# A gated two-branch attention on one core: a scheduled program replaced by one in a stored order, with fewer vector steps and transposes made by DMA

## The chip, the cores and the metric

The kernel runs on one core of one Trainium2 chip. The metric is device microseconds of one execution; lower is better. The engines are named as the profile names them: PE (TensorE), ACT (ScalarE), DVE (VectorE), POOL (GpSimd) and SP, which here only issues DMAs.

## What is computed

Input `x` has 2048 tokens of 640 values; there are 32 heads of 20. Two branches read it and a sigmoid gate mixes them.

```python
# branch A: linear attention, features are softmax(+p) and softmax(-p) of p = head @ w_phi
phi_q = concat([softmax(pq), softmax(-pq)]); phi_k = concat([softmax(pk), softmax(-pk)])
kv = einsum('bhsf,bhsd->bhfd', phi_k, v); z = einsum('bhsf->bhf', phi_k)
a = (phi_q @ kv) / (phi_q . z + 1e-6)  -> @ wo
# branch B: 4 segments of 512 tokens; causal softmax attention inside each segment,
# and a memory M, z summed over the earlier segments with phi(t) = where(t > 0, t + 1, exp(t))
o = g_h * (phi(q) @ M) / (phi(q) . z + 1e-6) + (1 - g_h) * softmax(q k^T * scale + mask) @ v
M = M + phi(k)^T v; z = z + sum(phi(k))   -> @ wo
out = g * a + (1 - g) * b,   g = sigmoid(x . gate_w)
```

## The kernel before

The program is recorded first and issued afterwards. Each call of `Graph.op` (L107) records one operation with an engine or a choice of engines, a guessed duration, a priority `pr`, and the tiles that it reads and writes. `schedule` (L134) then walks the operations greedily: for each engine it takes the candidates that could start within 0.12 us of the earliest one and picks the lowest priority number. In the same walk it hands out the 8 PSUM banks and the SBUF slots. `emit` (L359) writes five instruction streams in that order and places the semaphore waits. Each engine issues its stream strictly in order, so an instruction that waits holds up all that stand behind it.

Work by stages, with the lines that the prediction speaks of:

- Setup (L593): SP transposes `x` and two slices of `wqkv` by DMA while they are loaded, in this order: segment 0 of `x`, `wkT`, the other three segments, `wqT`. ACT's queue loads the rest. `fuse` (L669) multiplies w_phi into the A weights.
- Branch B, four segments n (`b_proj`, L687): the q and k projections (L698, five matmuls of 512 columns for each chunk), the v projection (L719, L720), and a way through DRAM (`scr`) for 12 of every 32 rows, so that 8 head groups of 4 heads lie at partitions 0, 32, 64 and 96.
- For each of the 8 groups (`b_step`, L815): three bursts of logit matmuls (L830; key tile 0, then tiles 1 and 3, then tile 2), five exponentials of 1024 columns (L839, L858), four masks on POOL (L844), and 40 small matmuls with the values (L884). For segments 1 to 3 four more matmuls read the memory in the same step (L887), and `combine` (L893) makes five DVE steps out of it (L906, L908, L916, L930, L933).
- Memory keys (`b_mem`, L746): PE transposes k (L762), ACT and DVE make the features from PSUM (L765, L767, L769).
- Outputs of a segment (`b_out`, L938): PE transposes (L947) and an evacuation each (L682 on ACT, L683 on DVE).
- Branch A keys (`a_k`, `a_kv`): projections (L968, L969), exponentials (L975), a sum per head and its reciprocal (L981, L982), a normalisation on POOL or DVE (L983), the kv matmuls (L999), and a running sum over tokens on DVE (L1022, 64 partitions by 1280).
- Branch A queries (`a_q`, L1062): projections (L1072), exponentials of both signs (L1077), then for each token tile two halves. In each half the two signs are multiplied by kv into two PSUM banks (L1097) and six DVE steps (L1105, L1106, L1107, L1110, L1112, L1113) bring them to one denominator and add them. PE transposes the result (L1122).
- `final` (L1139, L1140): both branches times `Wo`, 512 and 128 columns at a time, and the output DMA.

The core of a branch B step, and of the two signs:

```python
p0 = burst([(0, 0)]); expair(p0, 0, 0); mask(0, ...)
p1 = burst([(1, 0), (3, 384)]); expair(p1, 512, 1); mask(1, ...); mask(3, ...)
p2 = burst([(2, 0)])                       # 256 of 512 columns of each bank used
```

## Time and profile before

| | us |
|---|---|
| median of 3 runs | 446.2 (442.15 to 446.68) |
| span of the profiled execution, first to last instruction | 441.5 |
| PE busy in that span | 335.6 |
| DVE busy | 287.6 |
| ACT busy | 274.3 |
| POOL busy | 131.0 |

The profile is of one execution. Of its own time the page gives the span; the three runs lie 0.65 to 5.2 us above it, the median 4.7. Busy time is the union of an engine's instructions. PE's includes the time in which its clock was granted at half rate.

### The profile page before, as it was taken

What the parts mean: (1) busy time and instruction counts of PE and PEld (TensorE: products, weight loads), DVE (VectorE), ACT (ScalarE), POOL (GpSimd) and SP (SyncE); (2) the same over time, 40 slices, a digit from 0 to 9 for tenths busy, and PEclk for the clock granted to TensorE, in tenths of its full rate; (3) what the DMA queues carried; (4) which work ended last, traced back from release to release, by engine and by line L of the source; (5) the groups of instructions that cost most, each with busy time, mean ns of one, the idle gap of its engine ahead of it and who ended that gap; (6) DMA issues with size and microseconds to landing.
All of it is one profiled execution on the core that took longest, in us unless ns stands there. A gap on an engine that the chain in (4) does not pass through costs nothing.

```text
span 441.5 us, 8777 instructions
## 1 busy us (share of the span) xinstructions
PE 335.6 (76%) x3716; PEld 197.5 (45%) x3762; DVE 287.6 (65%) x584; ACT 274.3 (62%) x356; POOL 131.0 (30%) x163
## 2 busy tenths in 40 slices
PE   0198889596697788686878797877898688867667
PEld 0144454443373446344336454544545364534343
DVE  1321597957866868799428878778733598648940
ACT  1147858565646874577594577678487846477622
POOL 8100643423414441655120122132222212142310
PEclk9999999888698898699689999799898859865569
DMA  8993100410000000044100014000000000000001
GB/s 223 275 189 44 48 3 3 78 27 0 1 16 1 1 0 16 2 150 75 31 0 3 0 25 97 16 16 16 16 30 4 1 1 31 16 15 2 1 1 59
DMA packets 25799, 16.97 MB, mean 38 GB/s; under 512 B 17665, under 2 KB 23585, under 8 KB 25761
## 3 DMA queue, kind: packets, MB, share of 16 engines
q1 hardware_dynamic: 23040, 13.11, 13.4%
q10 hardware_dynamic: 2624, 3.28, 2.3%
q8 instruction: 29, 0.48, 0.4%
q0 software_dynamic: 96, 0.04, 0.2%
q14 instruction: 10, 0.07, 0.1%
HBM read 6.92 MB, written 4.59 MB: 26 GB/s over the span
## 4 chain that ended last, share of the span: by engine, by line
PE 44%; DVE 38%; ACT 9%; DMA 3%; issue 3%; POOL 1%; SPq 1%; POOLq 0%; ACTq 0%
PE ps L698 7%; PE ps L1139 7%; PE ps L968 5%; DVE acc L1022 5%; PE ps L1072 5%; ACT expT L839 4%; PE ps L884 4%; DVE cb L930 4%; DVE z L981 3%; DMA wkT<-in_A_wqkv_dram 3%; PE ps L719 3%; PE ps L1140 2%; DVE W L1110 2%; DVE W L1107 2%; PE ps L830 2%
## 5 line engine op out<-in xcount | busy, mean ns | idle before, releaser
L844 POOL TENSOR_SCALAR_AFFINE_SELECT expT<-expT 128x512 bf16<-128x512 bf16 x128 | 88.9, 697 | 266.5 <-ACT expT L839 216.1
L839 ACT ACTIVATE expT<-ps 128x1024 bf16<-128x1024 f32 x128 | 124.3, 1023 | 31.7 <-PE ps L830 31.5
L884 PE MATMUL ps<-v1B,expT 128*128 128x21 bf16 x1280 | 42.3, 175 | 10.5 <-POOL expT L844 8.0
L698 PE MATMUL ps<-xT,WB 128*128 128x512 bf16 x188 | 49.1, 402 | 1.3 <-issue 0.5
L884 PEld LDWEIGHTS ps<-v1B,expT 128*128 128x128 bf16 x1280 | 39.5, 98 | 18.5 <-POOL expT L844 11.1
L830 PE MATMUL ps<-qk 20*128 20x128 bf16 (+3 forms) x512 | 38.8, 338 | 8.8 <-ACT expT L839 5.8
L858 ACT ACTIVATE expT<-ps 128x1024 bf16<-128x1024 f32 x32 | 32.7, 1022 | 10.9 <-PE ps L830 10.9
L983 POOL TENSOR_TENSOR E<-E,z 128x1280 bf16<-128x1280 bf16 x12 | 30.0, 2496 | 21.9 <-DVE z L982 19.0
L1022 DVE TENSOR_TENSOR acc<-acc,E 64x1280 bf16<-64x1280 bf16 x31 | 31.6, 1018 | 0.8
L968 PE MATMUL ps<-WvA,xT 128*128 128x512 bf16 x74 | 26.7, 443 | 4.7 <-DVE cb L930 3.3
L1072 PE MATMUL ps<-xT,WqA 128*128 128x512 bf16 x95 | 27.9, 443 | 2.8 <-ACT expT L858 1.1
L698 PEld LDWEIGHTS ps<-xT,WB 128*128 128x128 bf16 x200 | 19.0, 102 | 23.1 <-issue 6.0
L1077 ACT ACTIVATE ET<-ps 128x512 bf16<-128x512 f32 x40 | 23.2, 600 | 8.5 <-PE ps L1072 8.1
L1097 PE MATMUL ps<-KVZ,ET 128*128 128x154 bf16 x192 | 20.7, 262 | 9.7 <-DVE W L1110 4.5
L682 ACT ACTIVATE out<-ps 128x640 bf16<-128x640 f32 x13 | 9.2, 704 | 29.5 <-PE ps L1140 29.5
L975 ACT ACTIVATE E<-ps 128x640 bf16<-128x640 f32 x32 | 22.6, 707 | 7.3 <-PE ps L969 7.0
L981 DVE TENSOR_REDUCE z<-E 128x64 f32<-128x1280 bf16 x16 | 23.6, 1478 | 4.9 <-ACT E L975 4.7
L682 ACT ACTIVATE qk<-ps 128x512 bf16<-128x512 f32 x29 | 17.3, 599 | 14.4 <-PE ps L698 13.5
L968 PE MATMUL ps<-WkA,xT 128*128 128x512 bf16 x73 | 23.5, 403 | 3.2 <-DVE vA L683 1.2
L1139 PE MATMUL ps<-Wo,oTA 128*128 128x512 bf16 x71 | 24.1, 422 | 1.1 <-DVE W L1110 1.1
L719 PE MATMUL ps<-WvB,xT 128*128 128x512 bf16 x75 | 23.5, 394 | 1.9 <-ACT v1B L682 1.1
L830 PEld LDWEIGHTS ps<-qk 20*128 20x128 bf16 x512 | 10.5, 94 | 31.7 <-ACT expT L839 13.2
(119 smaller groups left out, 655.5 us busy)
## 6 DMA issues: line engine op xcount, KB each, us to landing
out_dram<-out SPq DMA_DIRECT2D x16, 160.0 KB, 3.4
scr<-qk SPq DMA_DIRECT2D x16, 120.0 KB
qk<-scr SPq DMA_DIRECT2D x16, 120.0 KB
stq<-in_B_wq_dram ACTq DMA_DIRECT2D x1, 800.0 KB, 4.8
stk<-in_B_wk_dram ACTq DMA_DIRECT2D x1, 800.0 KB, 9.6
WvB<-in_B_wv_dram ACTq DMA_DIRECT2D x1, 800.0 KB, 11.6
...
```

Of the source, the lines that this page charges most:

```text
L698: r = e.matmul(self.pf(pt, 0, 0, LSEG), lhsT=self.WB[:, w, kc, 128 * c:128 * (c + 1)], rhs=xT[:, kc, LSEG * n:LSEG * (n + 1)], start=(kc = ...
L719: e.matmul(self.pf(pt, 0, 0, 512), lhsT=l, rhs=self.WvB[:, kc, 0:512], start=(kc == 0), stop=(kc == 4))
L830: r = e.matmul(self.pf(pt, i, c0, N), lhsT=qk[32 * i:32 * i + DH, g, 1, 128 * j:128 * (j + 1)], rhs=qk[32 * i:32 * i + DH, g, 0, 128 * j:L ...
L839: self.op("act", d_act(1024), lambda e, p=p: e.activation(ex[:, 2 * p:2 * p + 2, off:off + 512], self.pbanks(pt, 2 * p, 2, 512), ACT.Exp, ...
L844: self.op("pool", d_pool(n_el), lambda e: e.affine_select(view(), view(), pattern=pat, compare_op=ALU.is_ge, fill=0.0, base=0, channel_mul ...
L858: return e.activation(ex[:, :, 1024:1280].rearrange("p (k b) c -> p k b c", k=2), src, ACT.Exp, scale=scale)
L884: r = e.matmul(self.pf(ad, b, 84 * q2 + 21 * i, 21), lhsT=ex[:, i, c0:c0 + 128], rhs=vt[:, j, h, :], start=(j == 0), stop=(j == qi), skip_ ...
L968: e.matmul(self.pf(pt, 0, 0, 512), lhsT=l, rhs=W[:, kc, 0:512], start=(kc == 0), stop=(kc == 4))
L981: self.op("dve", d_dve(1280), lambda e: e.tensor_reduce(z[:, :], Ev(), axis=AX.X, op=ALU.add), R=[(E, 0), (E, 1)], W=[(z, "*")], claim=[rz ...
L1022: self.op("dve", d_dve(1280, 2), lambda e, src=src: e.tensor_tensor(acc[lo:lo + 64, :], acc[lo:lo + 64, :], src(), ALU.add), R=[(self.Et[t ...
L1072: r = e.matmul(self.pf(pt, 0, 0, LSEG), lhsT=self.WqA[:, kc, 128 * c:128 * (c + 1)], rhs=xT[:, kc, LSEG * S:LSEG * (S + 1)], start=(kc == ...
L1139: e.matmul(self.pf(pt, 0, 0, 512), lhsT=l, rhs=self.Wo[:, c, 0:512], start=(c == 0), stop=(c == 9))
```

## The change

The whole program is written anew. What it does, part by part:

- **Order.** `schedule` and all guessed durations are gone. `replay` takes three tables: `ORDER` (the 1317 operations in one sequence), `ENGINE` (which engine each operation with a choice gets) and `PLACE` (the PSUM banks and SBUF slots). The waits follow from the dependences as before.
- **Start.** Twelve matmuls on a zero tile come first on PE. SP's first transfer is segment 1 of `x`, and PE's first real work is its v projection; the B weights are rearranged in 20 small copies on DVE, ACT and POOL.
- **Key tile 2** of two head groups goes in one burst (`b_pair`), into one 512-column bank per head: two exponentials of 1024 columns and one mask of 1024 for both groups; tiles 1 and 3 share one mask. 80 bursts and 80 masks stand in place of 96 and 128.
- **Memory.** It is read once per token tile for all heads (`b_ret`), with three DVE steps and one addition on DVE or POOL, no longer in each group's step. The head gate sits in the mask `Mm` and in the ones column of the values, so the group's step keeps two DVE instructions.
- **Transposes by DMA.** The memory keys (15 transfers of 128x512), the outputs of branch B (16 of 128x640) and of branch A (16 of 128x640) are turned by transfers on SP's queue. The 256 PE transposes and their evacuations are gone.
- **Branch A's signs in one tile.** 40 matmuls with a 0/1 matrix sum the exponentials per head, DVE divides the two sums, the quotient is spread over the rows of its head through DRAM (four writes and one read on SP), and the negative sign's exponentials are multiplied by it. Both signs then add up in one PSUM tile; three DVE steps per token tile stand in place of twelve.
- **Running sum.** The token sums of branch A are done per sign (64 partitions by 640), and 31 of 64 go to POOL. The gate `1 - g` is applied in the output's evacuation.

```diff
-    def schedule(self):
-        free = {s: 0.0 for s in STREAMS}
-        bank_occ = [None] * 8
...
+    def replay(self, order, engine, place):
+        assert sorted(order) == list(range(len(self.ops)))
+        self.order = [self.ops[i] for i in order]
+        for p, o in enumerate(self.order):
+            o.pos = p
+            o.stream = o.engs[0]
+        for o, e in zip([o for o in self.ops if len(o.engs) > 1], engine):
+            o.stream = o.engs[e]
+        for o in self.order:
...
+                pl = place[t.idx]
+                if t.pool == "psum":
+                    t.t = list(pl)
...
-        p0 = burst([(0, 0)])
-        expair(p0, 0, 0)
-        mask(0, lambda: ex[:, :, 0:128], [[0, 4], [1, 128]], 512, [(0, 0), (0, 1)])
-        p1 = burst([(1, 0), (3, 384)])
-        expair(p1, 512, 1)
-        mask(1, lambda: ex[:, :, 512:640], [[0, 4], [1, 128]], 512, [(1, 0), (1, 1)])
-        mask(3, lambda: ex[:, :, 896:1024], [[0, 4], [1, 128]], 512, [(1, 0), (1, 1)])
...
-        self.op("act", d_act(1024), exp2, W=[(p2, i) for i in range(4)] + [(ex, 2)], pr=s + 0.02, name="exp2")
...
+    def b_pair(self, n, ga, gb):
+        exC = self.sbt("exC", [128, 4, 2, 256], BF16, self.p_exC)
+        pc = self.burst(n, [(ga, 2, 0), (gb, 2, 256)])
+        self.expm(pc, lambda p: exC[:, 2 * p:2 * p + 2, :, :].rearrange("p h g c -> p h (g c)"), exC, "c",
+                  (lambda: exC[:, :, :, 0:128], [[0, 4], [0, 2], [1, 128]]))
+        for k, g in enumerate((ga, gb)):
+            ex = self.sbt("exA", [128, 4, 1024], BF16, self.p_exA)
+            p0 = self.burst(n, [(g, 0, 0)])
+            self.expm(p0, lambda p, ex=ex: ex[:, 2 * p:2 * p + 2, 0:512], ex, "a", (lambda ex=ex: ex[:, :, 0:128], [[0, 4], [1, 128]]))
+            p1 = self.burst(n, [(g, 3, 0), (g, 1, 128)])
+            self.expm(p1, lambda p, ex=ex: ex[:, 2 * p:2 * p + 2, 512:1024], ex, "b",
+                      (lambda ex=ex: ex[:, :, 512:768].rearrange("p h (k c) -> p h k c", k=2), [[0, 4], [0, 2], [1, 128]]))
+            self.b_value(n, g, k, ex, exC)
+
...
-                    if am:
-                        r = e.matmul(self.pf(ad, b, 168 + 84 * q2, 84), lhsT=pqi[0][:, pqi[1], 128 * qi:128 * (qi + 1)],
-                                     rhs=self.Mzb[(n - 1) % 2][:, g, :], start=True, stop=True, skip_group_check=True)
...
+            self.op("dve", "mre", lambda e, U=U, r=r: e.tensor_scalar(r[:, :, :], U()[:, :, :, DH], 1e-6, None, op0=ALU.add), W=[(pt, 0), (r, "*")])
+            self.op("dve", "mrr", lambda e, r=r: e.reciprocal(r[:, :, :], r[:, :, :]), W=[(r, "*")])
+            self.op("dve", "mrm", lambda e, U=U, r=r, aM=aM: e.tensor_tensor(
+                aM[:, :].rearrange("p (b h d) -> p b h d", b=2, d=DH), U()[:, :, :, 0:DH],
+                r[:, :, :].rearrange("p b (h o) -> p b h o", o=1).to_broadcast([128, 2, 16, DH]), ALU.mult),
+                R=[(r, "*")], W=[(pt, 0), (aM, "*")])
+            self.op(("dve", "pool"), "aMadd", lambda e, q=q, aM=aM: e.tensor_tensor(self.oB[n][:, q, :], self.oB[n][:, q, :], aM[:, :], ALU.add),
+                    R=[(aM, "*")] + [(self.oB[n], g) for g in range(NG)], W=[(self.oB[n], ("t", q))])
...
-                    r = e.transpose(self.pb(pt, 0, 128 * g, 128), qk[:, g, 1, 128 * tl:128 * (tl + 1)], self.ident[:, :])
...
+        for c in range(NCH):
+            self.dma("sp", "ktr", lambda c=c: kt[:, :, 128 * c:128 * (c + 1)], qk[:, c, 1, :], R=[(qk, c)], W=[(kt, c)], transpose=True)
...
-                    r = e.transpose(self.pb(pt, 0, 128 * c, 128), oB[:, qi, 128 * c:128 * (c + 1)], self.ident[:, :])
-            self.op("pe", 5 * 0.065, tr, R=[(oB, (g, qi // 2)) for g in range(NG)] + [(self.ident, "*")], W=[(pt, 0)], claim=[oT], pr=pr, name="oTBtr")
-            self.evac(640, lambda oT=oT: oT[:, :, :], lambda pt=pt: self.pb(pt, 0, 0, 640).rearrange("p (c s) -> p c s", s=128),
-                      W=[(pt, 0), (oT, "*")], pr=pr, name="oTB_ev")
...
+            self.dma("sp", "oTB", lambda oT=oT: oT[:, :, :], lambda q=q: oB[:, q, :], R=[(oB, ("t", q))] + [(oB, g) for g in range(NG)],
+                     W=[(oT, "*")], transpose=True)
...
-                op("dve", 0.27, lambda e, U=U, sm=sm: e.reciprocal(sm[:, 0, :], U(1)[:, :, 21]), W=[(pt, 1), (sm, 0)], pr=p2, name="Uc")
-                op("dve", 0.2, lambda e, U=U, sm=sm: e.tensor_tensor(sm[:, 1, :], U(0)[:, :, 21], sm[:, 0, :], ALU.mult), R=[(sm, 0)], W=[(pt, 0), (sm, 1)], pr=p2, name="Uc")
-                op("dve", d_dve(336, 1, True), lambda e, U=U, sm=sm, W=W: e.tensor_tensor(
-                    W[:, :, :], U(1)[:, :, 0:21], sm[:, 1, :].rearrange("p (h o) -> p h o", o=1).to_broadcast([128, 16, 21]), ALU.mult),
...
+        def sums(e):
+            for s in range(2):
+                for c in range(NCH):
+                    for k in range(4):
+                        r = e.matmul(self.ps[32 * k:32 * k + 32, 512 * ss.t[0] + 128 * s:512 * ss.t[0] + 128 * s + 128], lhsT=Mo[:, c, :],
+                                     rhs=ET[:, s, c, 128 * k:128 * (k + 1)], start=(s == 0 and c == 0), stop=(c == 4),
+                                     tile_position=(0, 32 * k), skip_group_check=True)
+            return r
...
+        self.op("dve", "srec", lambda e: e.reciprocal(rb[:, :], self.pf(ss, 0, 128, 128)), W=[(ss, 0), (rb, "*")])
+        self.op("dve", "srat", lambda e: e.tensor_tensor(rr[:, :], self.pf(ss, 0, 0, 128), rb[:, :], ALU.mult), R=[(rb, "*")], W=[(ss, 0), (rr, "*")])
+        sc = self.scq[S % 2]
+        sp = self.sbt("sp", [128, NCH, LSEG], BF16, self.p_f)
+        for k in range(4):
+            self.dma("sp", "rw", sc.t.rearrange("(h d) (k t) -> k h d t", d=DH, k=4)[k],
+                     lambda k=k: rr[32 * k:32 * k + 32, :].rearrange("p (o t) -> p o t", o=1).to_broadcast([32, DH, 128]), R=[(rr, "*")], W=[(sc, k)])
+        self.dma("sp", "rd", lambda: sp[:, :, :], sc.t.rearrange("(c p) t -> p c t", p=128), R=[(sc, "*")], W=[(sp, "*")])
+        for cs in parts:
+            self.op(("dve", "pool"), f"Esc{len(cs)}", lambda e, cs=cs: e.tensor_tensor(
+                ET[:, 1, cs[0]:cs[-1] + 1, :], ET[:, 1, cs[0]:cs[-1] + 1, :], sp[:, cs[0]:cs[-1] + 1, :], ALU.mult), R=[(sp, "*")], W=[(ET, (1, cs[0]))])
+        kall = [(K1, ("z", s, c)) for s in range(2) for c in range(NCH)] + [(K1, ("kv", 0)), (K1, ("kv", 1))]
...
+            self.op("dve", "Ur", lambda e, U=U, r=r: e.reciprocal(r[:, :, :], U()[:, :, :, DH]), W=[(pt, 0), (r, "*")])
...
+            self.op("dve", "Uo", lambda e, U=U, r=r, oA=oA: e.tensor_tensor(
+                oA[:, :].rearrange("p (b h d) -> p b h d", b=2, d=DH), U()[:, :, :, 0:DH],
+                r[:, :, :].rearrange("p b (h o) -> p b h o", o=1).to_broadcast([128, 2, 16, DH]), ALU.mult),
+                R=[(r, "*")], W=[(pt, 0), (oA, "*")])
+            oT = self.sbt("oTA", [128, NCH, 128], BF16, self.p_oTA)
+            self.dma("sp", "oTA", lambda oT=oT: oT[:, :, :], lambda oA=oA: oA[:, :], R=[(oA, "*")], W=[(oT, "*")], transpose=True)
+            self.oTA[t] = oT
...
-                    self.op("dve", d_dve(1280, 2), lambda e, src=src: e.tensor_tensor(acc[lo:lo + 64, :], acc[lo:lo + 64, :], src(), ALU.add),
-                            R=[(self.Et[t], 0), (self.Et[t], 1)], W=[(acc, hf)], pr=pr, name="chain")
...
+                        self.op(("dve", "pool"), "chain", lambda e, src=src, s=s, lo=lo: e.tensor_tensor(acc[lo:lo + 64, s, :], acc[lo:lo + 64, s, :], src(), ALU.add),
+                                R=R, W=[(acc, (hf, s))], part=64 + hf)
...
+ORDER = """
+8 37 4 42 38 41 40 6 5 39 61 13 62 63 73 3 64 65 15 14 1 2 24 27 16 33 66 44 26 67 45 68 46 69 59 17 11 70 18 47 48 49 311 312 20 50 51 52 0 151 19 53
...```

SP at the start of the program, before (`xT` is the turned input, `wkT` and `wqT` the turned weights of branch A):

```order
L585 DMA_TRANSPOSE xT<-in_A_x_dram 128x5x512
L585 DMA_TRANSPOSE wkT<-in_A_wqkv_dram 128x5x640
L585 DMA_TRANSPOSE xT<-in_A_x_dram 128x5x512 x3
L585 DMA_TRANSPOSE wqT<-in_A_wqkv_dram 128x5x640
L590 DMA scr<-qk_55 12x5x1024 [waits prog_act]
```

Now (`kt` are turned memory keys; `WvA` stood on ACT's queue before):

```order
L382 DMA_TRANSPOSE xT<-in_A_x_dram 128x5x512
L386 DMA WvA<-in_A_wqkv_dram 128x5x640
L382 DMA_TRANSPOSE xT<-in_A_x_dram 128x5x512
L382 DMA_TRANSPOSE wkT<-in_A_wqkv_dram 128x5x640
L382 DMA_TRANSPOSE xT<-in_A_x_dram 128x5x512
L382 DMA_TRANSPOSE wqT<-in_A_wqkv_dram 128x5x640
L382 DMA_TRANSPOSE kt_99<-qk_56 128x4x128 [waits prog_act]
L382 DMA_TRANSPOSE xT<-in_A_x_dram 128x5x512
L386 DMA scr<-qk_56 12x5x1024 [waits prog_dve]
```

PE's first real matmul, of the v projection (L536), waits for the first transfer of this queue and the first of ACT's; before it was `fuse` (L669), behind the second. A transpose of memory keys, which waits for ACT, now stands ahead of the last segment of `x`.

SP in the middle of the program, before (`out_dram` is the output, `scr` and `qk` the way through DRAM):

```order
L590 DMA scr<-qk_55 12x5x1024 x3
L590 DMA qk_55<-scr 20x3x1024 [waits dma_sp_9,dma_sp_8,dma_sp_10,dma_sp_11]
L590 DMA qk_55<-scr 20x3x1024 x3
L590 DMA out_dram<-out_265 128x640 [waits prog_act]
L590 DMA scr<-qk_56 12x5x1024 [waits prog_act]
```

SP where the first two query segments of branch A pass, now (`scq` is the DRAM tile of the quotient, `oTA` and `oTB` are turned outputs):

```order
L386 DMA sp_216<-scq 128x5x512 [waits dma_sp_18,dma_sp_17,dma_sp_19,dma_sp_0]
L382 DMA_TRANSPOSE oTA_221<-oA_218 128x5x128 [waits dma_sp_5,prog_dve]
L382 DMA_TRANSPOSE oTA_222<-oA_220 128x5x128 [waits prog_dve]
L382 DMA_TRANSPOSE oTB_225<-oB_141 128x5x128
L382 DMA_TRANSPOSE oTA_228<-oA_224 128x5x128 [waits prog_dve]
L386 DMA scq<-rr_235 640x1x128 [waits dma_sp_9,prog_dve]
L386 DMA scq<-rr_235 640x1x128 x3
L386 DMA sp_237<-scq 128x5x512 [waits dma_sp_10,dma_sp_9,dma_sp_11,dma_sp_12]
```

SP's stream has 132 DMAs instead of 60, and one queue carries transposes, quotients and outputs in turn.

POOL where branch A's keys pass, before (L983 normalises, L844 masks):

```order
L983 TENSOR_TENSOR E_131<-E_131,z_136 128x1280 [waits prog_dve]
L844 AFFINE_SELECT expT_138<-expT_138 128x4x128 [waits prog_act] x2
L844 AFFINE_SELECT expT_138<-expT_138 128x4x128 [waits prog_pool]
L983 TENSOR_TENSOR E_135<-E_135,z_144 128x1280 [waits prog_dve]
L844 AFFINE_SELECT expT_138<-expT_138 128x4x128 [waits prog_act]
```

Now, where they pass, with the running sum (L763) between masks (L641):

```order
L763 TENSOR_TENSOR acc<-acc,E_89 64x640 [waits prog_pool]
L763 TENSOR_TENSOR acc<-acc,E_96 64x640 [waits prog_pool]
L763 TENSOR_TENSOR acc<-acc,E_91 64x640 [waits prog_pool]
L763 TENSOR_TENSOR acc<-acc,E_93 64x640 [waits prog_pool]
L763 TENSOR_TENSOR acc<-acc,E_109 64x640 [waits prog_dve]
L641 AFFINE_SELECT exA_122<-exA_122 128x4x128 [waits prog_pool,prog_act]
L763 TENSOR_TENSOR acc<-acc,E_109 64x640 [waits prog_pool]
L641 AFFINE_SELECT exA_125<-exA_125 128x4x256 [waits prog_pool,prog_act]
```

POOL now carries 71 two-input operations where it had 13, and they stand between the masks that PE waits for.

## Rows read from the trace of the kernel before

**Rows 1.** The page, busy time, share of the span and instructions of each engine.

```profile
PE 335.6 (76%) x3716; PEld 197.5 (45%) x3762; DVE 287.6 (65%) x584; ACT 274.3 (62%) x356; POOL 131.0 (30%) x163
```

**Rows 2.** Windows of 20 us: busy us and counts by engine, PEclk, DMA share, GB/s.

```profile
0.00:20.00 20.00, 0.04 (x1) 0.07 (x2) 6.00 (x15) 1.51 (x2) 10.56 (x22) 1.00 0.99 250
20.00:40.00 20.00, 19.79 (x108) 10.07 (x111) 2.70 (x4) 10.33 (x19) 0.00 (x0) 1.00 0.66 134
...
60.00:80.00 20.00, 17.51 (x235) 10.88 (x241) 16.71 (x29) 14.80 (x20) 5.76 (x7) 1.00 0.05 11
...
400.00:420.00 20.00, 13.88 (x182) 8.28 (x182) 17.57 (x49) 13.69 (x16) 6.83 (x11) 0.50 0.00 1
420.00:440.00 20.00, 15.28 (x142) 9.88 (x144) 4.40 (x9) 4.91 (x7) 1.20 (x2) 0.80 0.07 25
```

**Rows 3.** The page, chain that ended last, by engine.

```profile
PE 44%; DVE 38%; ACT 9%; DMA 3%; issue 3%; POOL 1%; SPq 1%; POOLq 0%; ACTq 0%
```

**Rows 4.** The same chain in order of time: start us, us, what.

```profile
5.74 14.09 DMA wkT<-in_A_wqkv_dram
...
66.89 1.08 PE ps L698 x5
...
145.04 1.00 PE ps L884 x40
...
152.92 2.25 PE ps L698 x5
```

**Rows 5.** Groups by line and shape: busy us, mean ns of one, idle before.

```profile
L839 ACT ACTIVATE expT<-ps 128x1024 bf16<-128x1024 f32 x128 | 124.3, 1023 | 31.7 <-PE ps L830 31.5
L844 POOL TENSOR_SCALAR_AFFINE_SELECT expT<-expT 128x512 bf16<-128x512 bf16 x128 | 88.9, 697 | 266.5 <-ACT expT L839 216.1 <-ACT expT L858 39.6 <-ACT eg L723 8.4
...
L983 POOL TENSOR_TENSOR E<-E,z 128x1280 bf16<-128x1280 bf16 x12 | 30.0, 2496 | 21.9 <-DVE z L982 19.0 <-DVE eg L730 2.8
...
L682 ACT ACTIVATE qk<-ps 128x512 bf16<-128x512 f32 x29 | 17.3, 599 | 14.4 <-PE ps L698 13.5 <-PE ps L1097 0.9
...
L769 DVE TENSOR_TENSOR pk<-pk,tmp 128x1024 bf16<-128x1024 bf16 x12 | 8.5, 711 | 0.3
...
L683 DVE COPY oTA<-ps 128x640 bf16<-128x640 bf16 x13 | 6.3, 487 | 4.3 <-PE ps L1122 4.1
```

**Rows 6.** DVE in order of time, half a token tile of branch A, first and last of six.

```profile
409.02 0.26 DVE L1105 RECIPROCAL as<-ps 128x16 f32<-128x16 f32 x1
...
410.89 0.55 DVE L1113 SCALAR_TENSOR_TENSOR oA<-W,g,as 128x320 bf16<-128x320 f32 x1
```

**Rows 7.** DVE in order of time, one group of branch B with memory, four of five.

```profile
422.77 0.35 DVE L908 RECIPROCAL cs<-cs 128x32 f32<-128x32 f32 x1
423.16 0.20 DVE L916 TENSOR_TENSOR cs<-cs,cf 128x32 f32<-128x32 f32 x1
423.40 0.82 DVE L930 TENSOR_TENSOR cb<-ps,cs 128x640 bf16<-128x640 f32 x1
424.26 0.33 DVE L933 TENSOR_TENSOR oB<-cb 128x320 bf16<-128x320 bf16 x1
```

**Rows 8.** DVE and POOL at 101 us; min/median/max ns of L1022 and L844.

```profile
101.33 2.32 DVE L917 TENSOR_TENSOR cs<-cs,cf 128x16 f32<-128x16 f32 x1
...
101.27 2.35 POOL L983 TENSOR_TENSOR E<-E,z 128x1280 bf16<-128x1280 bf16 x1 [2.08 <-DVE z L982]
...
L1022 DVE TENSOR_TENSOR acc<-acc,E x31: 805/823/2864, 58.7 to 208.3; 64x1280 bf16<-64x1280 bf16 x31
...
L844 POOL TENSOR_SCALAR_AFFINE_SELECT expT<-expT x128: 630/637/1930, 42.4 to 420.7; 128x512 bf16<-128x512 bf16 x128
```

**Rows 9.** SP's queue by line: issue time ns min/median/max.

```profile
L585 SPq DMA_TRANSPOSE xT<-in_A_x_dram x4: 2967/3200/4872, 0.8 to 23.2; - x4
...
L585 SPq DMA_TRANSPOSE wqT<-in_A_wqkv_dram x1: 3777/3777/3777, 26.3 to 26.3; - x1
...
L590 SPq DMA_DIRECT2D out_dram<-out x16: 332/332/367, 259.1 to 439.2; - x16
```

More of the change, by code (lines that the diff above doesn't have):

```diff
@@ L127, in op @@
         o.stream = None
-        o.succ = []
         o.inc = False
@@ L368, in emit @@
                 allsem[("q", q, i)] = qsem[q][i]
+        last = None
         for o in self.order:
             ds = dict.fromkeys(o.deps)
+            if o.stream == "pool" and not o.dma:
+                if last is not None and last.part != o.part:
+                    ds[last] = None
+                last = o
             for t in o.tiles:
-                if any(w[0] is t for w in o.writes):
+                if t in o.writes:
                     for d in t.prev:
@@ L1149, in build_all, with build @@
+    def build(self):
+        self.Et, self.vt, self.oTB, self.oTA, self.oB = [], [], {}, {}, {}
         self.setup()
```

1218 lines of the change are left out of this document (467 added, 751 removed), and 47 rows, old and new, of tables (ORDER, PLACE).

## The prediction

> **What bounds the kernel now.** I read the busy shares first, then the 20 us windows, then the chain of waits, and last the groups by line. No engine is full: PE is busy 76% of the span, DVE 65%, ACT 62%, POOL 30% [rows 1]. The windows say how far that is from a bound. In each of the 22 windows I take the engine that is busiest there; these maxima add up to 364 of 440 us (first and last window, with the worst one for the clock, in [rows 2]). So for 17% of the time not even the busiest engine of the moment works: the engines wait for each other in streams that are strictly in order. The chain that ended last is 44% PE, 38% DVE and 9% ACT [rows 3], so time leaves this kernel through PE and DVE work, and through fewer handovers between them. Two more things stand in the windows. PE does nothing in the first 20 us [rows 2], because its first matmul waits for `wkT`, which lands at 19.83 us [rows 4]. And the granted clock is not constant: five matmuls of 512 columns take 1.08 us at the 2.4 GHz level and 2.25 at the 1.2 GHz level [rows 4]; it is 1.00 in 60 to 80 us, where PE is busy 17.5 of 20, and 0.50 in 400 to 420 [rows 2], where PE stops and starts between small pieces.
>
> **Part by part, engine by engine.**
>
> *DVE.* Branch A's half tile takes six instructions, from 409.02 to 411.44: 2.4 us, 32 times, 77 us [rows 6]. In its place come, per token tile, a reciprocal of 32, a scaling and a 640 product: 0.35 + 0.20 + 0.82 [rows 7], 16 times, 22 us; and per segment the quotient (two instructions on 128 columns, about 1.2, worked out from 0.35 for 32) and part of the scaling of the negative sign (0.7 per 1024 columns [rows 5]), together about 9. That saves 46. `combine` with memory takes five instructions, the last four from 422.77 to 424.59, so 2.0 us in all, 24 times, 49 us [rows 7]; two of them (0.25 + 0.5) remain in all groups, and the memory read adds 12 times 1.4 us and three additions: 49 goes, 36 comes, 13 saved. The evacuations of turned tiles go: 20 of 0.49 [rows 5], 10 us. The features of keys and queries become six long pairs from SBUF where 24 short pairs stood, about 14 saved. Half of the running sum goes to POOL, about 16 saved. Against this DVE evacuates 14 of the 20 doubled q and k tiles, 8 us more, and takes evacuations of v and of the output from ACT (15 of 0.8) and small steps of the setup, 17 more. Counting all 400 instructions at such prices I get 214 us instead of 288.
>
> *ACT.* The 160 exponentials stay, 1024 columns each at 1.02 us [rows 5]: 164 us by mean, 4% less by union. Gone are 12 evacuations of turned tiles, and 29 evacuations of 0.6 us [rows 5] become 6 of 1.02. I get 254 by means, 245 by union, instead of 274.
>
> *PE.* Removed are 256 transposes of 128 columns, 33,000 columns; some 5,000 others fall away in smaller matmuls, and 6,000 (the first twelve), 4,000 (memory) and 5,000 to 20,000 (the sums, by whether four column parts run side by side, which no row shows) come in. The balance is 3 to 23 thousand columns, 1 to 10 us at 1.08 us per 2560. The whole new stream has 490,000 columns, 207 us at that price, 32 times 1.00 us with the values [rows 4] and 41,000 columns of logits, four parts abreast, 17 us: 256. I add a tenth for the gaps before small matmuls and take 283. The other end is today's 335.6 less 8: 328, if the clock stays as uneven as it is.
>
> *POOL.* Masks keep their elements but come in 80 pieces where 128 of 0.70 us [rows 5] stood: between 56 us, if only their number counted, and 89, if only their columns did; I take 78. The normalisation costs half of 2.5 us [rows 5], 1.25, per 640 columns, 20 times; the running sum, priced alike though it covers 64 partitions, 29 times; 22 other two-input operations about 30 us. Sum 182 instead of 131. Between 0.41 (half of DVE's 823 ns [rows 8]) and 1.25 for a sum on POOL, I take the nearer row, which is POOL's own.
>
> *SP and the transfers.* A 640-column transpose of 512 rows takes 2.97 to 3.2 us of the queue, one of 640 rows 3.78 [rows 9]: 0.75 us per 128 rows. 47 new ones are then 35 us of queue time, the 20 transfers for the quotient some 10, and the whole queue 92 us of some 350. No row shows a transpose out of SBUF; the ends are 0.33, a plain transfer of one tile, and 2.97 [rows 9]; 0.75 lies near the first, and scales the second by size. In the last stretch one such trip, about 3 us with landing, replaces five PE transposes and an evacuation of 0.49 [rows 5]: some 2 us more at the very end.
>
> **The sum.** I cut the new order at its 32 value steps, add up each engine's work in each of the 33 pieces, and take the largest: 309 us in all, PE or ACT in three pieces out of four, never SP. Means overlap by 3 to 4% in a busy union, as for the exponentials above, so 300. Before these pieces lie the first transfers, which no longer include `wkT`: 8 us instead of 20 (not before 5.7, when SP's queue is through with its first transfer, and not after the 19.8 of `wkT` [rows 4]). After them lies the end: 6 us for the last turn and the last output. What remains is how often the busiest engine of a piece runs. It is 0.83 today [rows 2]. The new order puts other work in front of each wait (the branch A half of `final` stands before the half that needs the turned output, two query segments before the read of the quotient), and the pieces are half as long, so I take 0.90: 300 / 0.90 + 14 = 347 us of span. At 0.83 it is 375, at 1.0 it is 314. The runs before lie 0.7 to 5.2 us above the span of 441.5, their median 4.7; with 3 for that I forecast 350 us.
>
> **The rivals.**
>
> *The port.* DVE and POOL hold each other up: an addition of 16 columns on DVE took 2.32 us beside a POOL product that ran from 101.27 to 103.62, and the running sum, 823 ns in the middle, reached 2864; POOL's mask, 637 in the middle, reached 1930 [rows 8]. With 71 two-input operations on POOL instead of 13, some 80 DVE operations with two SBUF inputs meet a busy POOL 52% of the time (182 of 350) and wait half of 1.25 us: 25 us; in return POOL waits about 9. DVE has room for its 25 (239 of 350), so I count a third of the 34 within the 0.90. If all 34 lie on the chain, the time is 350 + 23 + as much again for PSUM banks freed late and a PE that falls to its lower clock: 396 at most, about 385. The Trainium skill, "SBUF — State Buffer", section "SBUF: two separate sides", calls the pair of ports that the two share an exclusive lock: "the other fully blocks". The trace agrees: the 2.32 us ends when POOL's 2.35 us end. It speaks against moving the running sum to POOL.
>
> *The order misses.* It was fixed by durations that the chip need not keep. If the busiest engine runs 0.83 of its time as today: 375 + 3 = 378. For it: 47 transfers of a kind with no row; against it: two engines now carry nearly all pieces.
>
> *The queue, and slower than before.* If a transpose out of SBUF costs the queue 2.97 us whatever its size, 47 of them cost 140 us instead of 35, and every quotient and output waits behind them: 350 + 104 = 454. From 2.9 us each it is slower than today. Against it: issue time goes with size between 512 and 640 rows [rows 9], 3.2 to 3.78.
>
> *Better.* PE keeps its upper clock all through, as in 60 to 80 us [rows 2], and the order holds: 314 + 3 = 317.
>
> **Chances.** The forecast, 350 with its own range of 335 to 368: 0.57. The port, 385: 0.13. The order misses, 378: 0.13. Better, 317: 0.12. The queue, 454: 0.05. The range that leaves out two in ten runs from 322, short of the best case, to 392, past port and order. Slower by over 1% is the queue alone, 0.05; a result within 1% (about what a measurement of this kernel can tell from no change) needs the queue at just under 2.9 us each, 0.02; faster is the rest, 0.93.
>
> **What would show it.** Right: DVE near 214 to 240 busy, ACT near 245, PE under 310; PE's first matmul of the v projection at 7 to 13 us; a clock of 0.9 or more; PE the largest part of the chain and DVE under 25% of it; transposes on SP at 0.6 to 1.0 us of issue. Wrong: PE idle before the value steps for POOL's masks, with running sums in front of them on POOL; DVE additions of 16 or 32 columns at over 1 us in their mean; SP's queue busy over 150 us, or PE's waits named after `oTA`, `oTB` or the quotient.

## The result, and the profile after

| | before | after |
|---|---|---|
| median, on one chip, four runs each | 444.17 us (441.51 to 446.68) | 338.88 us (335.07 to 341.63) |
| span of the profiled execution | 441.5 | 336.2 |

The ratio is 0.7613, 95% interval 0.7549 to 0.7677: 24% faster. A ratio leaves out the runs that lie over 1.5% above the fastest of their kernel; the medians hold all runs. The forecast was 350, its own range 335 to 368.

The busy times, on the page of the changed kernel, answer to [rows 1]:

```profile
PE 298.2 (89%) x3726; PEld 188.0 (56%) x3726; DVE 243.9 (73%) x400; ACT 238.6 (71%) x276; POOL 196.8 (59%) x191
```

All work but POOL's shrank: DVE by 44 us, PE by 37, ACT by 36. The windows of 20 us, with columns as in [rows 2]:

```profile
0.00:20.00 20.00, 7.49 (x22) 2.90 (x22) 4.68 (x15) 4.08 (x8) 8.10 (x29) 0.83 0.97 235
20.00:40.00 20.00, 19.77 (x164) 13.03 (x165) 11.92 (x35) 13.46 (x21) 3.66 (x10) 1.00 0.52 112
...
120.00:140.00 20.00, 18.73 (x248) 12.03 (x246) 17.84 (x24) 18.32 (x19) 19.28 (x15) 1.00 0.27 52
...
200.00:220.00 20.00, 15.41 (x206) 8.01 (x205) 14.32 (x30) 12.98 (x14) 7.34 (x7) 0.83 0.43 120
...
300.00:320.00 20.00, 19.83 (x336) 15.22 (x335) 12.35 (x27) 11.60 (x14) 6.89 (x8) 1.00 0.30 78
320.00:340.00 20.00, 13.01 (x102) 9.05 (x99) 6.12 (x11) 2.16 (x3) 5.36 (x4) 0.94 0.43 88
```

The largest of PE, DVE, ACT and POOL in each of the 17 windows adds up to 303 of 336 us, a share of 0.90, where it was 364 of 440, 0.83. How large such a share is depends on the windows: in windows of 10 us it is 0.91 (307 us) and 0.88 (387 us). In the 15 windows between 20 and 320 us it is 281.6 of 300, 0.94; the worst of them is 200 to 220, where branch A's first quotient is made. From 120 to 140 all four engines work 18 to 19 of 20 us; no window of before shows that. The chain, by engine:

```profile
PE 51%; DVE 23%; DMA 10%; ACT 4%; issue 4%; SPq 4%; POOL 3%; ACTq 0%; DVEq 0%; POOLq 0%
```

Against [rows 3], DVE's share fell from 38 to 23%. DMA and SP's queue together rose from 4 to 14%: some 47 us of this chain are transfers and their issue. The chain in order of time, at the start, at branch A's last quotient and at the end:

```profile
0.81 4.85 SPq L382
5.73 0.82 SPq L386
6.60 13.58 DMA xT<-in_A_x_dram
...
281.21 4.04 DMA scq<-rr
285.26 5.05 DMA sp<-scq
290.38 1.12 issue
...
323.29 8.42 PE ps L878 x60
...
332.43 0.79 ACT out L394
```

The groups by line and shape that answer to the terms of the sum (columns as in [rows 5]):

```profile
L639 ACT ACTIVATE exA<-ps 128x1024 bf16<-128x1024 f32 x128 | 124.3, 1024 | 30.8 <-PE ps L628 30.2
L763 POOL TENSOR_TENSOR acc<-acc,E 64x640 bf16<-64x640 bf16 x29 | 46.3, 1600 | 10.4 <-DMA acc<-acc 5.3 <-DVE E L724 3.0
...
L763 DVE TENSOR_TENSOR acc<-acc,E 64x640 bf16<-64x640 bf16 x33 | 27.6, 846 | 0.9 <-POOL acc L763 0.2
L724 POOL TENSOR_TENSOR E<-E,z 128x640 bf16<-128x640 bf16 x20 | 26.1, 1314 | 3.1 <-DVE z L722 2.7
...
L861 DVE TENSOR_TENSOR oA<-ps,r 128x640 bf16<-128x640 f32 x16 | 13.1, 824 | 2.1 <-DMA oTA<-oA 1.0 <-ACT r L859 0.7
```

The sums on DVE hardly became cheaper: 27.6 us for 33 of half the columns, where 31 of the full 1280 took 31.6 before:

```profile
L1022 DVE TENSOR_TENSOR acc<-acc,E 64x1280 bf16<-64x1280 bf16 x31 | 31.6, 1018 | 0.8
```

And SP's transposes out of SBUF, by line (issue time ns min/median/max):

```profile
L382 SPq DMA_TRANSPOSE oTB<-oB x16: 1199/1276/2215, 106.3 to 327.5; - x16
L382 SPq DMA_TRANSPOSE oTA<-oA x16: 1199/1250/1712, 225.9 to 322.5; - x16
L382 SPq DMA_TRANSPOSE kt<-qk x15: 1190/1269/2094, 53.0 to 192.0; - x15
```

### The profile page after: what moved, and what is told of

It reads as the page before. It is cut to its first block, busy times and chain, and to the rows that moved or that the text cites. A ratio compares the mean times of both kernels' runs of the same rounds, so it can differ in the third digit from the quotient of the medians.

```text
span 336.2 us, 8681 instructions
## 1 busy us (share of the span) xinstructions
PE 298.2 (89%) x3726; PEld 188.0 (56%) x3726; DVE 243.9 (73%) x400; ACT 238.6 (71%) x276; POOL 196.8 (59%) x191
## 4 chain that ended last, share of the span: by engine, by line
PE 51%; DVE 23%; DMA 10%; ACT 4%; issue 4%; SPq 4%; POOL 3%; ACTq 0%; DVEq 0%; POOLq 0%
PE ps L878 9%; PE ps L516 8%; PE ps L702 7%; PE ps L806 6%; PE ps L673 6%; DVE acc L763 5%; PE ps L628 4%; DMA xT<-in_A_x_dram 4%; PE ps L851 3%; DVE E L724 2%; SPq L386 2%; DMA qk<-scr 2%; ACT exA L639 2%; SPq L382 2%; POOL acc L763 2%
## 5 line engine op out<-in xcount | busy, mean ns | idle before, releaser
L639 ACT ACTIVATE exA<-ps 128x1024 bf16<-128x1024 f32 x128 | 124.3, 1024 | 30.8 <-PE ps L628 30.2
L641 POOL TENSOR_SCALAR_AFFINE_SELECT exA<-exA 128x1024 bf16<-128x1024 bf16 (+1 forms) x64 | 60.3, 950 | 74.2 <-ACT exA L639 73.2
L763 POOL TENSOR_TENSOR acc<-acc,E 64x640 bf16<-64x640 bf16 x29 | 46.3, 1600 | 10.4 <-DMA acc<-acc 5.3
L628 PE MATMUL ps<-qk 20*128 20x384 bf16 (+3 forms) x512 | 32.8, 309 | 12.9 <-DVE aM L612 3.8
L673 PEld LDWEIGHTS ps<-v1B,exA 128*128 128x128 bf16 x1024 | 35.8, 96 | 5.5 <-issue 1.3
L673 PE MATMUL ps<-v1B,exA 128*128 128x21 bf16 x1024 | 37.2, 173 | 1.3 <-POOL exA L641 0.6
L639 ACT ACTIVATE exC<-ps 128x1024 bf16<-128x1024 f32 x32 | 31.3, 1025 | 8.8 <-PE ps L628 8.8
L516 PEld LDWEIGHTS ps<-xT,WB 128*128 128x128 bf16 x200 | 18.5, 101 | 23.2 <-issue 5.8
L641 POOL TENSOR_SCALAR_AFFINE_SELECT exC<-exC 128x1024 bf16<-128x1024 bf16 x16 | 19.8, 1238 | 15.0 <-ACT exC L639 14.9
L763 DVE TENSOR_TENSOR acc<-acc,E 64x640 bf16<-64x640 bf16 x33 | 27.6, 846 | 0.9 <-POOL acc L763 0.2
L724 POOL TENSOR_TENSOR E<-E,z 128x640 bf16<-128x640 bf16 x20 | 26.1, 1314 | 3.1 <-DVE z L722 2.7
L878 PE MATMUL ps<-Wo,oTA 128*128 128x320 bf16 x160 | 25.5, 310 | 2.1 <-DVE out L395 2.1
L628 PEld LDWEIGHTS ps<-qk 20*128 20x128 bf16 x512 | 9.2, 92 | 32.1 <-issue 12.4
L702 PE MATMUL ps<-WkA,xT 128*128 128x320 bf16 x160 | 25.7, 310 | 1.5 <-DVE qk L395 1.5
## 6 DMA issues: line engine op xcount, KB each, us to landing
stk<-in_B_wk_dram ACTq DMA_DIRECT2D x1, 800.0 KB, 13.1
```

Of the source, the lines that this page charges most:

```text
L516: r = e.matmul(self.pf(pt, w, 0, LSEG), lhsT=WB[:, w, kc, 128 * c:128 * (c + 1)], rhs=xT[:, kc, LSEG * n:LSEG * (n + 1)], start=(kc == 0), ...
L628: r = e.matmul(self.pf(pts[i // 2], i % 2, c0, N), lhsT=qk[32 * i:32 * i + DH, g, 1, 128 * j:128 * (j + 1)], rhs=qk[32 * i:32 * i + DH, g, ...
L639: self.op("act", "exp", lambda e, p=p: e.activation(view(p), self.pbanks(pts[p], 512), ACT.Exp, scale=scale), W=[(pts[p], 0), (t, (key, p))])
L641: self.op("pool", "mask" + str(len(pat)), lambda e: e.affine_select(mv(), mv(), pattern=pat, compare_op=ALU.is_ge, fill=0.0, base=0, chann ...
L673: r = e.matmul(self.pf(pt, 0, 84 * q + 21 * i, 21), lhsT=src(j, i, q), rhs=vt[:, j, head_of(g, i), :], start=(j == 0), stop=(j == q), skip ...
L702: r = e.matmul(self.pf(pt, b, 0, 320), lhsT=l, rhs=W[:, kc, 320 * b:320 * b + 320], start=(kc == 0), stop=(kc == 4))
```

## The experiments

There are twelve runs. "Ratio" is always to the kernel before on the same chip, with its 95% interval; the changed kernel has 0.7613 (above) and 0.7636 (0.7578 to 0.7693) in its second set of runs.

| run | median us | ratio |
|---|---|---|
| e1 new work, old rules of order | 422.31 | 0.9498 (0.9445 to 0.9550) |
| e2 before, with 32 turned outputs by DMA | 443.62 | 1.0003 (0.9965 to 1.0041) |
| e3 running sum all on DVE | 347.21 | 0.7798 (0.7753 to 0.7843) |
| e4 each transpose twice | 371.07 | 0.8356 (0.8298 to 0.8413) |
| e5 47 more transposes of a fixed tile | 371.19 | 0.8353 (0.8299 to 0.8406) |
| e6 v weights later | 338.86 | 0.7624 (0.7575 to 0.7672) |
| e7 quotient's transfers first | 338.12 | 0.7631 (0.7601 to 0.7662) |
| e8 first matmuls cut | 339.23 | 0.7648 (0.7606 to 0.7691) |
| e9 old rules' order, moved | 381.12 | 0.8583 (0.8513 to 0.8653) |
| e10 sum on DVE, moved | 342.39 | 0.7693 (0.7640 to 0.7746) |
| e11 the changed kernel again | 340.84 | 0.7636 (0.7578 to 0.7693) |
| e12 queue relieved | 338.40 | 0.7578 (0.7516 to 0.7641) |

### Is it the work or the order? (e1, e9)

The first question is which of the two moved the time. `e1` keeps every operation of the changed kernel and makes the order anew with the greedy rule of before (`schedule`), its priority formulas and filler limits. Where an operation is new, I gave it the priority of the one that it replaces. So it imitates the old rules, and is not the old scheduler itself.

```diff
-ORDER = 8 37 4 42 38 41 40 6 5 39 61 13 62 63 73 ...      (the stored order)
+ORDER = 0 1 13 4 37 14 2 6 3 38 15 5 39 40 44 ...         (the old rules; 127 of 248 digits of ENGINE and 452 of 620 entries of PLACE differ too)
```

> The changed kernel's 1317 operations, unchanged, in an order made by the greedy rules and priority formulas of the kernel before (with mean durations as the two traces show them); only the three tables differ. If the new order carries much of the gain: 375 to 400 us, since the busiest engine of the moment would then run 0.8 to 0.85 of its time, with DVE, ACT and POOL as busy as now (240, 239, 190 to 200). If the smaller work carries it alone: 336 to 348.

Measured: 422.31 us. Busy times and chain of its page:

```profile
PE 318.7 (76%) x3726; PEld 199.4 (47%) x3726; DVE 240.5 (57%) x406; ACT 252.6 (60%) x293; POOL 174.6 (41%) x168
...
PE 43%; DVE 25%; DMA 14%; ACT 10%; SPq 3%; POOL 2%; issue 2%; POOLq 0%
```

DVE works 240 us, as little as in the changed kernel, and yet the program is only 5% faster than before. The maxima by window add up to 353 of 422 us, 0.84. So smaller work under the old rules left both numbers of the old program nearly as they were: the share stayed (0.83, 0.84), and the maxima themselves stayed long (364, 353). PE alone is busy for 336, 319 and, in the changed kernel, 298 us; the maxima exceed that by 28, 34 and 5. So under the old rules other engines than PE were often the busiest, as in these windows of `e1` (columns as in [rows 2]):

```profile
200.00:220.00 20.00, 9.12 (x165) 7.12 (x166) 17.23 (x23) 11.22 (x13) 14.70 (x12) 0.77 0.45 118
...
380.00:400.00 20.00, 11.88 (x214) 7.47 (x211) 8.45 (x15) 17.73 (x20) 11.81 (x11) 0.53 0.24 67
```

The time was even above the range that I expected of order (375 to 400).

`e9` starts from that order, moves single operations and changes 109 engine choices; banks and buffers stay as they are in `e1`.

```diff
-ORDER = 0 1 13 4 37 14 2 6 3 38 15 5 39 40 44 ...
+ORDER = 0 39 1 2 13 44 3 6 18 20 16 4 14 32 41 ...       (109 of 248 digits of ENGINE differ too)
```

> The changed kernel's operations in the order by the old rules (422 us), improved by many small moves of single operations and 109 other engine choices of 248, without a new plan and without other banks or buffers. If order is what the 422 us lack: the time falls well below them, to 365 to 400, with the busy times of all engines within 10 us of the 319, 240, 253 and 175 there and the share of the busiest engine up from 0.84. If something else in that program costs the time (banks, buffers, the queue): 410 to 425.

Measured: 381.12 us. Its page:

```profile
PE 306.5 (81%) x3707; PEld 192.7 (51%) x3726; DVE 242.9 (64%) x407; ACT 239.2 (63%) x275; POOL 192.9 (51%) x185
```

The time fell by 41 us, as expected of order; PE lost 12 us, ACT 13, and POOL gained 18, more than the 10 that I had allowed. By windows of 20 us the share did not rise as I had expected: the maxima are 320 of 378 us, still 0.85, and what fell is their sum, from 353. Cut at the starts of the 32 value steps, the share is 0.90 (324 of 361 us of PE's time from first to last real matmul), where `e1` has 0.86 (345 of 402). Moves and engine choices alone, without a new plan for banks and buffers, give back about half of what separates `e1` from the changed kernel. Roughly, then, and by the ratios (0.950, 0.858, 0.764), the 105 us of the change are 22 for the work under old rules, 41 for local moves, and 42 for the rest of the stored order with its engine choices, banks and buffers. How the three split depends on how well `e1` imitates the old rules, and on the work being counted first: the old work in a new order was not run, so what an order alone would give it stays open.

### One part of the work alone (e2)

The kernel before gets the turned outputs by transfer, nothing else; its own scheduler makes the order.

```diff
-            self.op("pe", 5 * 0.065, tr, R=[(oA, 0), (oA, 1), (self.ident, "*")], W=[(pt, 0)], claim=[oT], pr=pru + 0.5, name="oTAtr")
-            self.evac(640, lambda oT=oT: oT[:, :, :], ...)
+            self.dma("sp", lambda oT=oT: oT[:, :, :], lambda oA=oA: oA[:, :], R=[(oA, 0), (oA, 1)],
+                     W=[(oT, "*")], pr=pru + 0.5, nbytes=100e3, transpose=True, name="oTAtr")
```

> The kernel before, with one part of the change alone: its 32 turned outputs (both branches) by transfers out of SBUF, not by five PE transposes and an evacuation each; its own scheduler makes the order. If this part gains what the prediction's terms say (160 PE transposes and 32 evacuations of 0.5 to 0.6 us less, some 10 us of PE and 17 of DVE and ACT, at a share of 0.83): 430 to 440 us. If the work was hidden and each turn is only late by its landing time: 441 to 448. If the queue holds everything up: over 455.

Measured: 443.62 us, ratio 1.0003. The page's busy times:

```profile
PE 334.4 (75%) x3602; PEld 188.3 (42%) x3602; DVE 279.2 (63%) x565; ACT 264.7 (59%) x342; POOL 131.0 (29%) x164
```

The 17 us of DVE and ACT went as the terms say (287.6 to 279.2 and 274.3 to 264.7). PE's busy time hardly fell (335.6 to 334.4), but the profiled execution had its clock at 0.858 instead of 0.872: busy time times clock went from 293 to 287. The time did not move at all; it lies in the range for work that was hidden and turns that are late by their landing. Part of what left shows as waiting on ACT (who waited for whom, us, times, longest), with 52.1 us where the kernel before had 29.5 (its line is L1140 there):

```profile
ACT out L682 <- PE ps L1127: 52.1, 14, 11.7
```

Some became landing: at the end of the program 2.6 us of the chain (from 426.5 us) are the transfer of a turned `oTB`, which PE waits for. The run doesn't tell the two apart.

### POOL's sums and the shared port (e3, e10)

`e3` tests the rival on the port: the whole running sum goes to DVE, at the places that the stored order has for it.

```diff
 engine of "chain" and "chain0" (L761, L763):
-dve 33, pool 31
+dve 64
```

> The changed kernel with its whole running sum on DVE (31 engine choices of 248 differ). By the theory that the shared port makes both engines pay: a sum on DVE falls from its mean of 846 ns to 420 to 550, DVE stays within 5 us of 244 though it has 31 sums more, POOL falls from 197 to about 150, and the time falls by 1 to 2%, to 331 to 336 us. By the theory that POOL's work lay beside the path: 337 to 341. If DVE is the bound in the middle of the program and sums keep their 846 ns: DVE 268, 345 to 352.

Measured: 347.21 us, slower by some 2%, in the range that I had given for another cause (DVE as the bound, at 268 us busy). The busy times of the page, and the sums from the answer on that line:

```profile
PE 301.8 (87%) x3726; PEld 188.8 (55%) x3726; DVE 247.3 (71%) x431; ACT 238.6 (69%) x276; POOL 148.2 (43%) x160
...
L763 DVE TENSOR_TENSOR acc<-acc,E x62: 420/489/1572, 68.4 to 204.1; 64x640 bf16<-64x640 bf16 x62
```

The busy times came as the port theory said: DVE 247.3 with 31 sums more, POOL 148.2. The sums fell less than it said: 489 ns is their median, their mean 666, where I had 420 to 550. So two engines together had 45 us less to do, and the program was longer. The chain of `e3` shows where (start us, us, what):

```profile
126.11 1.94 DVE acc L763 x2
128.07 1.45 DVE acc L763
129.55 0.49 DVE acc L763
130.06 0.48 DVE acc L763
130.55 0.75 DVE vA L395
131.29 0.14 issue
131.43 0.61 PE ps L628 x7
```

Five sums in a row stand in DVE's stream in front of the evacuation of `vA`, and PE goes on only behind that. The stored order had put all five on POOL. `e10` keeps all sums on DVE and moves operations, in the way of `e9`; the longest rows of sums become 4, 3 and 3 where they were 9, 5 and 4.

```diff
 DVE's stream, lengths of the longest rows of sums:
-9 5 4 4 4
+4 3 3 2 2
```

> The changed kernel with the whole running sum on DVE, as in the run at 347 us, but with single operations moved in the order; the longest rows of sums on DVE's stream are 4, 3 and 3 where they were 9, 5 and 4. If the sums were slow only because they stood in front of evacuations that PE waits for: 333 to 341 us with DVE still near 247 and POOL near 148. If the sums cost DVE too much wherever they stand: 344 to 350.

Measured: 342.39 us beside 340.84 of `e11`, the changed kernel again.

> The changed kernel again, beside the two others on the same chip: 337 to 341 us; any run of the others within 1% of it counts as the same.

The 342.39 of `e10` lies between its two ranges. The intervals of `e10` and `e3` don't overlap, those of `e10` and `e11` do: most of the 8 us was the place of the sums and of what stands around them. The same moves with the sums left on POOL were not run. That the sums take long beside POOL even so can be read from `e10`:

```profile
L763 DVE TENSOR_TENSOR acc<-acc,E x62: 418/490/1569, 58.9 to 202.8; 64x640 bf16<-64x640 bf16 x62
```

Of its 36 sums that have other work of DVE before and behind them, 12 met no work on POOL and took 0.47 to 0.49 us each; 24 met some and took 0.42 to 1.55, 0.97 in the mean.

### SP's queue (e4, e5, e7, e12)

`e4` issues each transpose out of SBUF a second time, right behind the first, into a spare tile.

```diff
+            x = self.op(q, "twice", lambda e: e.dma_start_transpose(jk[:, 0:n, :], i() if callable(i) else i), R=R, dma=True)
```

> The changed kernel with each of the 47 transposes out of SBUF issued a second time into a spare tile right behind the first: 47 times 1.27 us more on SP's queue, 60 us. If the queue has room, as the prediction says: 337 to 344 us. If the queue is near the path: 350 to 365, with PE waits that go back to the quotient, the turned outputs or the memory keys.

Measured: 371.07 us, above both ranges, so my own side of it, "the queue has room", is wrong. The chain of its page, and the longest wait on a spare copy:

```profile
PE 42%; DVE 22%; DMA 17%; SPq 11%; issue 3%; POOL 2%; ACT 2%; ACTq 0%; DVEq 0%; POOLq 0%
```

```profile
DVE oA L880 <- DMA junk<-oA: 15.8, 6, 4.9
```

The second row leaves a doubt: the second copy also holds branch A's output buffer longer. `e5` takes it away: the same number of transposes at the same places, but of a tile of weights that nobody changes.

```diff
-            x = self.op(q, "twice", lambda e: e.dma_start_transpose(jk[:, 0:n, :], i() if callable(i) else i), R=R, dma=True)
+            x = self.op(q, "more", lambda e: e.dma_start_transpose(jk[:, :, :], self.WvB[:, 0, 0:D]), R=[(self.WvB, "w")], dma=True)
```

> The changed kernel with 47 more transposes on SP's queue, at the same places as the second ones before, but their source is a fixed tile of weights, so that no output buffer is held longer; each waits for the landing of the one before it, as they share a spare tile. If the 32 us of the run with second transposes came from the queue itself: 362 to 380 us. If they came from output tiles of branch A held longer (DVE waited 15.8 us for them there): 340 to 352.

Measured: 371.19 us, the same. So it was the queue and not the held buffers. Its row for the added transposes (issue ns):

```profile
L402 SPq DMA_TRANSPOSE junk<-WvB x47: 1199/1269/2323, 56.1 to 365.1; - x47
```

47 times 1.27 is 60 us of queue and 32 us of time: 0.7 us for each one that is added, about half of the time that it holds the queue. Of the queue's waits 7.2 us are for the spare tile. The data that the additions move are not what slowed it: branch A's turned outputs landed 2.6 us after their issue and held the queue for 1.22 us in the median, where the changed kernel has 2.7 and 1.25.

Does less on the queue pay too? In the changed kernel the four writes of the last quotient are split by a turned output and a read, and the chain above runs through them from 281 to 290 us. `e7` puts them together:

```diff
 SP, last query segment:
-scq<-rr x3, oTA, qk<-scr, scq<-rr, oTB, sp<-scq
+scq<-rr x4, oTA, qk<-scr, sp<-scq, oTB
```

> The changed kernel with two places of SP's queue altered in branch A's last query segment: the fourth write of the quotient right behind the third, ahead of a turned output and a read of the way through DRAM, and the read of the quotient ahead of a turned output of branch B. The chain goes through this trip from 277.8 to 290.4 us. If it is on the path: the read lands 3 to 4 us earlier and the time falls by 2 to 4 us, to 335 to 337. If PE has other work there: 338 to 340.

Measured: 338.12 us, ratio 0.7631. The chain of `e7` in that stretch is PE alone:

```profile
280.34 0.33 PE ps L628 x8
280.67 1.46 PE ps L878 x10
...
290.59 1.47 PE ps L878 x10
...
297.99 0.36 PE ps L628 x8
```

The trip has left the chain, and in the profiled executions the 40 value matmuls behind it start 10.5 us after the 40 before them, where it was 14.0 (291.89 to 302.42, and 288.85 to 302.87). But the trip itself began 3.0 us later in that execution (first write at 280.24, where it was 277.20), so its read was issued at 285.09, where it was 285.26. The median doesn't show the 3.5 us; whether the later start is the price of the move or lies within the spread of the runs stays open. `e12` adds two more reliefs.

```diff
+        self.dma("act" if t in (0, 3, 4, 5, 13, 14, 15) else "sp", "out", ...)
-        self.dma("sp", "out", ...)
 and the orders of e6 and e7
```

> The changed kernel with SP's queue relieved in three places: the v weights' load later and the quotient's writes together, as in the two runs before, and the seven outputs that ACT evacuates issued by ACT right behind the evacuation. SP waited 9.6 us in all for such evacuations, with turned outputs behind it in the queue; 60 us more on the queue cost 32. If less on the queue pays in the same measure: 330 to 336 us. If the order left the queue just enough room: 336 to 341, the same as now.

Measured: 338.40 us, ratio 0.7578, within 1% of the changed kernel, and its interval overlaps that one's. More on the queue costs; for less these runs show no gain, and one below 1% they could not show.

### The start (e6, e8)

```diff
 SP, first transfers:
-xT (segment 1), WvA, xT (segment 0), wkT, ...
+xT (segment 1), xT (segment 0), wkT, WvA, ...
```

> The changed kernel with the load of branch A's v weights (800 KB) put behind the second segment of the input and the k weights on SP's queue. If the first loads are bound by what they move together (235 GB/s in the first 20 us): the second segment lands some 3 us earlier than at 20.2, PE's second v projection starts at about 17 us, and the time falls by 1 to 3 us, to 336 to 338. If the start is hidden by the two segments already at work: 338 to 340.

Measured: 338.86 us, ratio 0.7624: no change. PE at the start, first in the changed kernel, then in `e6` (start us, us, what, idle before):

```profile
4.69 4.65 PE L427 MATMUL ps<-zero 128*128 128x512 bf16 x12 [4.69 <-DVE zero L421]
15.36 0.42 PE L536 MATMUL ps<-WvB,xT 128*128 128x320 bf16 x1 [6.01 <-DMA xT<-in_A_x_dram]
...
20.23 0.31 PE L536 MATMUL ps<-WvB,xT 128*128 128x320 bf16 x1 [2.04 <-DMA xT<-in_A_x_dram]
```

```profile
15.88 0.42 PE L536 MATMUL ps<-WvB,xT 128*128 128x320 bf16 x1 [5.89 <-DMA xT<-in_A_x_dram]
...
18.88 0.45 PE L536 MATMUL ps<-WvB,xT 128*128 128x320 bf16 x1 [0.17 <-DMA xT<-in_A_x_dram]
```

The second segment comes 1.35 us earlier, not 3, and the first is no earlier (15.88, where it was 15.36). `e8` cuts the twelve matmuls on zeros to three of 16 columns:

```diff
-                for _ in range(4):
-                    r = e.matmul(self.pf(pt, 0, 0, 512), lhsT=ze[:, 0:128], rhs=ze[:, :], start=True, stop=True)
+                r = e.matmul(self.pf(pt, 0, 0, 16), lhsT=ze[:, 0:128], rhs=ze[:, 0:16], start=True, stop=True)
```

> The changed kernel with the twelve matmuls on zeros cut to three of 16 columns. The first ten real matmuls take 0.47 us each although the twelve ran before them (0.30 later), so the twelve seem to give nothing: 338 to 340 us and the same 0.47. If they do keep PE's clock up later: 341 to 343.

Measured: 339.23 us, no change; its first real matmul is as slow:

```profile
15.37 0.43 PE L535 MATMUL ps<-WvB,xT 128*128 128x320 bf16 x1 [10.43 <-DMA xT<-in_A_x_dram]
```

## Why the prediction was right, point by point

**The sum.** I wrote 300 / 0.90 + 14 = 347 us of span. Measured: 336.2, of which 15.4 lie ahead of PE's first real matmul and 4.5 behind the last of the chain (323.29 + 8.42 = 331.7). Cut at the starts of the 32 value steps, as the prediction's pieces were, the 316 between hold 298 us of the busiest engine, 0.94. So the 300 was right within 1%, the share was too low by 0.04 (worth 17 us), and the start too early by 7.4. The 300 is in part luck: DVE had 30 us more to do than priced, PE and POOL 15 each. And part of the step from 0.83 to 0.90 was the cut: at its value steps the kernel before has 0.86 already (361 of 419 us); 0.83 holds for windows of 20 us.

**The start: wrong by the size of a term.** I took 8 us, with first matmuls at 7 to 13; they came at 15.36. SP's queue is through with the first transpose at 5.66 as before, but PE waits for its data until 15.36. In the first 20 us the transfers of all queues move 235 GB/s together and the DMA engines are busy at 0.97; `WvB`, `stq` and `stk` on ACT's queue are among them. That these hold the first segment up was not tested; `e6` shows that the load behind it in SP's own queue has no part in the first matmul's time.

**DVE: mis-sized.** Forecast 214, measured 243.9, just outside the 214 to 240 that I called right. The largest step that I can name is "Half of the running sum goes to POOL, about 16 saved": it saved 4, because the 33 sums took 846 ns each in the mean. Nine of them met no work on POOL and took 0.42 to 0.49 us; the other 24 took 0.98. Waits of this kind stand in the prediction as the port's 25 us, outside the 214; with them it had 239. Of the new per-tile steps the product came as priced (`oA` 0.82, 16 times), the scaling did not (0.56 in the mean for 14, instead of 0.20: 5 us). The other 13 of the 30 us I have not taken apart.

**ACT and PE: right.** ACT 238.6, forecast 245. PE 298.2 at a mean granted clock of 0.949, forecast 283 at the upper clock. The two products, 298.2 x 0.949 = 283 and 335.6 x 0.872 = 293, are rough, since the clock is a mean over the span; they say that PE's work shrank by 10 us, at the end of the 1 to 10, and that the rest of its 37 us is the clock. (The columns in the prediction add up to 8 to 23 thousand, not 3 to 23: 3 to 10 us.) The clock was higher where PE stopped less: 0.872 at 0.76 of the span busy before, 0.901 at 0.81 in `e9`, 0.949 at 0.89 now; `e10`, with 0.965 at 0.86, is out of this line. Which brings about which no run separates.

**POOL: near.** 196.8 for 182; the 29 sums took 46.3 us, 1.6 each, where I had 36. (The terms that the prediction names add up to 169; it doesn't say what the other 13 of its 182 are.)

**SP: the weakest step.** "0.75 lies near the first": a 128x640 transpose out of SBUF took 1.25, so 47 are 60 us and not 35. The queue's 132 issues took 134 us in all, not 92; the 150 that would have shown the prediction wrong were not reached. That this load had no price on the path was wrong too. It lies near it: `e5` gives 0.7 us of time for each transpose added. If that held all the way, which two points can't show, I estimate that the rival in which a transpose costs 2.97 (81 us of queue more than measured) would have come to some 382 us, not to 454, and that the change would lose from over 5 us each, not from 2.9.

**The port.** Its mechanism is there, in the trace of the changed kernel (POOL, then DVE; start us, us, what):

```profile
110.97 1.10 POOL L641 TENSOR_SCALAR_AFFINE_SELECT exC<-exC 128x1024 bf16<-128x1024 bf16 x1
111.02 1.39 DVE L763 TENSOR_TENSOR acc<-acc,E 64x640 bf16<-64x640 bf16 x1
```

The sum begins 0.05 us behind the mask and ends 0.34 behind the mask's end: beyond the 0.42 to 0.49 us that a sum takes alone, 0.9 to 1.0 of its 1.39 is waiting, nearly the whole mask. The rule of the Trainium skill that the prediction cited ("SBUF — State Buffer", section "SBUF: two separate sides") says that the one that comes second blocks until the first is done, and the trace agrees. What I took from it, that the running sum on POOL speaks against the change, was wrong: without it on POOL the time was the same at best (`e10`) and longer where the order wasn't made for it (`e3`).

**The order.** I held the sum of the pieces (300) and the share (0.90) for two separate numbers, and priced "the order misses" at 378 by the old share alone. `e1`, the same work in another order with other engine choices and places, shows 422: a worse order lowers the share and also lengthens the sum of the maxima, from 303 to 353. That the order would carry about four fifths of the gain (83 of 105 us, with the work counted first) was not in the prediction, whose main term was less work on DVE. `e2` shows that one part of this work, taken out of the old program alone, gave nothing. So the time was forecast well, and what makes it only in part.
